# Attention by chunks of 512 queries, with the mixer, MLP and next projections of a finished chunk scheduled under the next chunk

## The chip, the core and the metric

The kernel runs on one core of a Trainium2 chip. The metric is device time in microseconds (us). The profiles are single executions. PE is the matrix engine, ACT the engine of exponentials and Gelu, DVE the vector engine, GpSimd (POOL) does small work, SP issues transfers. Attention is called bare where no side work runs under it. PSUM is the memory that PE writes; a bank of it holds one score tile.

A ratio below is the mean time of one kernel's runs over that of the kernel before, both from the same rounds. It is therefore not quite the ratio of the medians that are quoted.

## The reference, cut to what matters

Four layers over 2048 tokens of width 512: attention, mixer with MLP, attention, mixer with MLP. Attention has 32 query heads of width 16 and a single key and value head.

```python
def _A_ref(x, wq, wk, wv, wo):                      # H = 32, Dh = 16
    q = ...; k = x @ wk; v = x @ wv                 # one K and V for all heads
    scores = jnp.einsum("bhqd,bkd->bhqk", q, k) * (Dh ** -0.5)
    p = _softmax(scores, axis=-1)
    o = jnp.einsum("bhqk,bkd->bhqd", p, v)
    return o... @ wo
def _B_ref(x, w1, w2, w3, w4):
    h = _gelu(_layernorm(x) @ w1)
    ...                                             # four column groups shifted by 1, -1, 2, -2 tokens
    x1 = x + hs @ w2
    return x1 + _gelu(_layernorm(x1) @ w3) @ w4     # F = 1792
x = x + _A_ref(_layernorm(x), ...); x = x + _B_ref(_layernorm(x), ...)   # twice
```

There are 32 heads x 4 query chunks x 16 key blocks x 2 layers = 4096 score tiles of 128 x 512 to exponentiate. That is the largest single piece of work. A chunk's mixer needs only two tokens beyond the chunk, and its MLP nothing; only attention needs all keys.

## The kernel before

It works layer by layer. An attention step is one key block of three heads: three score matmuls on separate row groups of PE into three PSUM banks, one exponential over 1536 columns, four value matmuls on separate column groups. Two score slots alternate. Side work (Q projections, output projections, normalization) is slipped in by a fixed budget, one item in each step, through one PSUM bank.

```python
SBANK = [[0, 1, 2], [3, 4, 5]]
ACCB = 6
aux = {'b': 7, 'rot': None, 'i': 0, 'xb': 7}
...
for n in range(N):
    p, heads, qsb, kb = steps[n]
    emit_exp(n)
    ...                                   # fillers up to FILL_BUDGET = 0.55
    emit_pv(n, kb == NKB - 1)
    if n + 2 < N:
        emit_scores(n + 2)
```

After the last head of the last chunk the mixer layer follows, over all 16 token tiles. Gelu is built from a copy, a square and a tanh on ACT and two products on DVE, so that the exponential's activation table can stay.

```python
if kind == 'A':   # ACT copy of PSUM      'B': ACT Square      'D': ACT Tanh
...
sc.op("DVE", lambda e: e.scalar_tensor_tensor(out=un['dest'], in0=tb3, scalar=1.0, in1=pb3,
                                            op0=ALU.add, op1=ALU.mult), ...)
```

The softmax here doesn't subtract the row's maximum and nothing guards it: scores larger than these inputs give would overflow.

Of the kernel before, what the change touches and what calls it, by code (L numbers as in the profile page):

```python
# [12 lines left out]
class Sched:  # L13
    def __init__(self, nc):
        self.nc = nc
        self.thunks = {e: [] for e in ENGINES}
        self.count = {e: 0 for e in ENGINES}
        self.sems = {}
        for e in ENGINES:
            self.sems[e] = nc.alloc_semaphore(f"s_{e}")  # L20
        self.waited = {e: {} for e in ENGINES}
        self.res = {}
        self.subs = {}
        self.psum = {}
        self.ndma = 0
        self.out_dma_toks = []

    def _merge(self, deps, tok):
        if tok is None:
            return  # L30
        k, v = tok
        if deps.get(k, -1) < v:
            deps[k] = v

    def _tag_records(self, tag):
        zone, cell, sub = tag
        keys = [(zone, cell, None)]
        if sub is None:
            for s in self.subs.get((zone, cell), ()):
                keys.append((zone, cell, s))  # L40
        else:
            keys.append((zone, cell, sub))
        return keys

    def _deps(self, eng, reads, writes, banks):
        deps = {}
        for t in reads:
            for key in self._tag_records(t):
                info = self.res.get(key)
                if info is not None:  # L50
                    self._merge(deps, info['w'])
        for t in writes:
            for key in self._tag_records(t):
                info = self.res.get(key)
                if info is not None:
                    self._merge(deps, info['w'])
                    for k, v in info['r'].items():
                        self._merge(deps, (k, v))
        for b in banks:
            prev = self.psum.get(b)  # L60
            if prev is not None and prev[0] != eng:
                self._merge(deps, prev[1])
        return deps

    def _record(self, eng, tok, reads, writes, banks):
        for t in writes:
            zone, cell, sub = t
            if sub is not None:
                self.subs.setdefault((zone, cell), set()).add(sub)
            self.res[t] = {'w': tok, 'r': {}}  # L70
            if sub is None:
                for s in self.subs.get((zone, cell), ()):
                    self.res[(zone, cell, s)] = {'w': tok, 'r': {}}
        for t in reads:
            zone, cell, sub = t
            if sub is not None:
                self.subs.setdefault((zone, cell), set()).add(sub)
            info = self.res.setdefault(t, {'w': None, 'r': {}})
            k, v = tok
            if info['r'].get(k, -1) < v:  # L80
                info['r'][k] = v
        for b in banks:
            self.psum[b] = (eng, tok)

    def _emit_waits(self, e, eng, deps):
        for k, v in sorted(deps.items(), key=lambda kv: str(kv[0])):
            if self.waited[eng].get(k, -1) >= v:
                continue
            e.wait_ge(self.sems[k], v)
            self.waited[eng][k] = v  # L90

    def op(self, eng, emit_fn, reads=(), writes=(), banks=(), extra=()):
        reads = tuple(reads)
        writes = tuple(writes)
        banks = tuple(banks)
        deps = self._deps(eng, reads, writes, banks)
        for tok in extra:
            self._merge(deps, tok)
        self.count[eng] += 1
        tok = (eng, self.count[eng])  # L100
        if deps.get(eng, -1) >= tok[1]:
            raise AssertionError("self dependency")

        def thunk(e, deps=deps, emit_fn=emit_fn, eng=eng):
            self._emit_waits(e, eng, deps)
            ins = emit_fn(e)
            ins.then_inc(self.sems[eng], 1)
        self.thunks[eng].append(thunk)
        self._record(eng, tok, reads, writes, banks)
        return tok  # L110

    def dma(self, emit_fn, reads=(), writes=(), eng="SP", out=False, extra=()):
        reads = tuple(reads)
        writes = tuple(writes)
        self.ndma += 1
        key = f"d{self.ndma}"
        sem = self.nc.alloc_semaphore(key)
        self.sems[key] = sem
        deps = self._deps(eng, reads, writes, ())
        for tok in extra:  # L120
            self._merge(deps, tok)

        def thunk(e, deps=deps, emit_fn=emit_fn, eng=eng, sem=sem):
            self._emit_waits(e, eng, deps)
            ins = emit_fn(e)
            ins.then_inc(sem, 16)
        self.thunks[eng].append(thunk)
        tok = (key, 16)
        if out:
            self.out_dma_toks.append(tok)  # L130
        for t in writes:
            zone, cell, sub = t
            if sub is not None:
                self.subs.setdefault((zone, cell), set()).add(sub)
            self.res[t] = {'w': tok, 'r': {}}
            if sub is None:
                for s in self.subs.get((zone, cell), ()):
                    self.res[(zone, cell, s)] = {'w': tok, 'r': {}}
        for t in reads:
            info = self.res.setdefault(t, {'w': None, 'r': {}})  # L140
            k, v = tok
            if info['r'].get(k, -1) < v:
                info['r'][k] = v
        return tok

    def finish(self, block):
        outs = list(self.out_dma_toks)

        def final_thunk(e):
            for key, v in outs:  # L150
                e.wait_ge(self.sems[key], v)
        self.thunks["SP"].append(final_thunk)

        def mk(eng):
            def f(e):
                for t in self.thunks[eng]:
                    t(e)
            return f
        if self.thunks["PE"]:
            block.tensor(mk("PE"))  # L160
        if self.thunks["ACT"]:
            block.scalar(mk("ACT"))
        if self.thunks["DVE"]:
            block.vector(mk("DVE"))
        if self.thunks["POOL"]:
            block.gpsimd(mk("POOL"))
        if self.thunks["SP"]:
            block.sync(mk("SP"))


CELL = 1024


class Zone:
    def __init__(self, nc, name, nbytes, stack):
        assert nbytes % CELL == 0
        self.name = name
        self.nbytes = nbytes
        self.t = stack.enter_context(
            nc.sbuf_tensor(name, [128, nbytes // 2], dt.bfloat16))  # L180

    def view(self, byte_off, shape, dtype):
        esz = dt.size(dtype)
        n = 1
        for s in shape:
            n *= s
        assert byte_off % 4 == 0 and (n * esz) % 2 == 0
        ap = self.t[:, byte_off // 2: byte_off // 2 + (n * esz) // 2]
        if dtype != dt.bfloat16:
            ap = ap.bitcast(dtype)  # L190
        if len(shape) == 1:
            return ap
        dims = " ".join(f"a{i}" for i in range(len(shape)))
        kw = {f"a{i}": shape[i] for i in range(1, len(shape))}
        return ap.rearrange(f"p ({dims}) -> p {dims}", **kw)

    def cells(self, byte_lo, byte_hi, sub=None):
        assert 0 <= byte_lo < byte_hi <= self.nbytes, (self.name, byte_lo, byte_hi)
        c0 = byte_lo // CELL
        c1 = (byte_hi - 1) // CELL  # L200
        return [(self.name, c, sub) for c in range(c0, c1 + 1)]


class Buf:
    def __init__(self, zone, byte_off, shape, dtype):
        self.zone = zone
        self.off = byte_off
        self.shape = tuple(shape)
        self.dtype = dtype
        self.esz = dt.size(dtype)  # L210
        n = 1
        for s in shape:
            n *= s
        self.ap = zone.view(byte_off, shape, dtype)
        self.nbytes = n * self.esz
        st = [1] * len(shape)
        for i in range(len(shape) - 2, -1, -1):
            st[i] = st[i + 1] * shape[i + 1]
        self.strides = st

    def tags(self, *idx, sub=None):
        n_elems = 1
        for s in self.shape:
            n_elems *= s
# [16 lines left out]
class ZoneAlloc:  # L241
# [5 lines left out]
    def buf(self, shape, dtype, align=None):  # L247
# [3 lines left out]
        for s in shape:  # L251
            n *= s
# [871 lines left out]
```

## Time and profile before

2651.01 us (median of three, 2647.76 to 2652.38).

The five stages of this run (head, attention, mixer and MLP, attention, mixer and MLP) are cut out and timed in the prediction.

The page's forty slices show the stages at a glance: each digit is a tenth of the slice, PEclk the granted clock of PE.

```profile
PE   5888889888888889457878888888888888893588
...
ACT  5899999999999997346658999999999999973474
...
PEclk8955555555555555578988555555555555555789
```

ACT is near full where PE runs at half clock, and falls to 3 to 6 tenths where neither attention runs. The further lines of this profile stand in the prediction.

### The profile page before, as it was taken

The numbers are of one execution on the slowest core, as the hardware profiler recorded it, in microseconds if no ns is written. First come the engines' busy times: TensorE is split into PE (matmuls) and PEld (weight loads), VectorE is DVE, ScalarE is ACT, GpSimd is POOL, SyncE is SP. The second block draws the span as 40 slices with busy tenths as digits, with TensorE's granted clock in tenths as the row PEclk, the third lists the DMA queues.
The fourth block names the chain that finished last, engine by engine and source line by source line (L and its number), as shares of the span: only waits on it lengthen the run. The fifth ranks groups of instructions, "written<-read, shape, count | busy, mean of one in ns | idle before, by whom it ended". The sixth has DMA issues, their size and how long they took to land.

```text
span 2650.2 us, 30433 instructions
## 1 busy us (share of the span) xinstructions
PE 2174.1 (82%) x12641; PEld 550.5 (21%) x12728; DVE 842.9 (32%) x1552; ACT 2179.0 (82%) x1689; POOL 70.5 (3%) x93
## 2 busy tenths in 40 slices
PE   5888889888888889457878888888888888893588
PEld 2211111111111111123332111111111111110243
DVE  5312122012122012677742121220122121127776
ACT  5899999999999997346658999999999999973474
POOL 2000000000000000030100000000000000000200
PEclk8955555555555555578988555555555555555789
DMA  1000000000000000100000000000000000001000
GB/s 49 17 1 1 1 1 1 1 1 1 1 1 1 1 1 1 56 1 1 9 9 16 1 1 1 1 1 1 0 1 1 1 1 1 1 1 56 0 1 32
DMA packets 15466, 17.74 MB, mean 7 GB/s; under 512 B 2528, under 2 KB 14304, under 8 KB 15328
## 3 DMA queue, kind: packets, MB, share of 16 engines
q1 hardware_dynamic: 15328, 15.80, 1.9%
q8 instruction: 99, 1.62, 0.3%
q14 instruction: 39, 0.32, 0.0%
HBM read 13.70 MB, written 2.10 MB: 6 GB/s over the span
## 4 chain that ended last, share of the span: by engine, by line
ACT 47%; PE 35%; DVE 13%; issue 5%; DMA 0%; ACTq 0%; DVEq 0%
ACT zT L727 43%; PE PB L752 10%; PE PB L709 8%; PE PB L1021 4%; PE PB L689 4%; DVE zC L411 3%; PE PB L610 2%; DVE zT L771 2%; PE PB L734 2%; PE PB L1042 2%; DVE zT L618 2%; ACT zT L911 2%; PE PB L994 1%; DVE zT L816 1%; DVE zX L693 1%
## 5 line engine op out<-in xcount | busy, mean ns | idle before, releaser
L727 ACT ACTIVATE zT<-PB 128x1536 bf16<-128x1536 f32 (+1 forms) x1408 | 1926.2, 1411 | 193.9 <-PE PB L709 188.2
L752 PE MATMUL PB<-zT 128*32 128x512 bf16 x5632 | 849.7, 594 | 224.5 <-ACT zT L727 187.6
L709 PE MATMUL PB<-zT 32*128 32x512 bf16 x4096 | 837.4, 589 | 1.6 <-DVE zT L618 1.6
L771 DVE CAST zT<-PB 128x512 bf16<-128x512 f32 x88 | 60.6, 689 | 1118.8 <-PE PB L752 1118.8
L752 PEld LDWEIGHTS PB<-zT 128*32 128x32 bf16 x5632 | 155.8, 101 | 780.1 <-ACT zT L727 638.5
L709 PEld LDWEIGHTS PB<-zT 32*128 32x128 bf16 x4096 | 146.5, 98 | 596.3 <-issue 593.8
L693 DVE TENSOR_TENSOR zX<-PB,zX 128x512 f32<-128x512 f32 x256 | 176.4, 689 | 204.5 <-PE PB L689 170.2
L816 DVE TENSOR_TENSOR zT<-zT,PB 64x512 bf16<-64x512 bf16 (+2 forms) x144 | 98.7, 685 | 180.8 <-PE PB L800 179.0
L484 PE MATMUL PB<-zC,zT 128*128 128x128 bf16 x384 | 36.7, 274 | 132.1 <-ACT zT L461 108.5
L1021 PE MATMUL PB<-zW,zT 128*128 128x512 bf16 x440 | 112.2, 411 | 29.8 <-DVE zT L921 29.0
L689 PE MATMUL PB<-zW,zT 128*128 128x512 bf16 x212 | 124.5, 604 | 8.5 <-DVE zX L693 8.1
L908 ACT ACTIVATE zT<-PB 128x1024 bf16<-128x1024 f32 x72 | 74.1, 1029 | 64.1 <-PE PB L1042 53.1
L914 DVE SCALAR_TENSOR_TENSOR zT<-zT 128x1024 bf16<-128x1024 bf16 x72 | 88.2, 1225 | 79.8 <-ACT zT L911 79.8
L461 ACT ACTIVATE zT<-zT,zC 128x512 bf16<-128x512 f32 (+1 forms) x40 | 28.7, 801 | 102.4 <-DVE zC L449 102.4
L1042 PE MATMUL PB<-zT,zW 128*128 128x512 bf16 x438 | 101.0, 379 | 5.9 <-ACT zT L908 5.4
L921 DVE SCALAR_TENSOR_TENSOR zT<-zT 128x1024 bf16<-128x1024 bf16 x72 | 88.0, 1223 | 0.1
L461 ACT ACTIVATE zT<-zX,zC 128x512 f32<-128x512 f32 (+1 forms) x24 | 17.2, 801 | 81.6 <-DVE zC L449 81.6
L918 ACT ACTIVATE zT<-zT 128x1024 bf16<-128x1024 bf16 x72 | 76.6, 1064 | 4.4 <-DVE zT L914 4.4
L911 ACT ACTIVATE zT<-zT 128x1024 bf16<-128x1024 bf16 x72 | 76.7, 1065 | 0.0
L610 PE MATMUL PB<-zT,zW 128*128 128x512 bf16 x239 | 65.1, 391 | 10.4 <-DVE zT L618 2.9
L734 PE MATMUL PB<-zC 16*128 16x512 bf16 x88 | 51.6, 586 | 25.6 <-DVE zT L771 25.6
L800 PE MATMUL PB<-zC,zT 128*128 128x128 bf16 x352 | 67.6, 296 | 2.4 <-DVE zT L789 2.4
(68 smaller groups left out, 765.6 us busy)
## 6 DMA issues: line engine op xcount, KB each, us to landing
zW<-in_B_w_dram SPq DMA_DIRECT2D x4, 1792.0 KB, 9.5
zT<-in_A_x_dram SPq DMA_DIRECT2D x4, 512.0 KB, 5.5
zW<-in_B_w_dram SPq DMA_DIRECT2D x4, 512.0 KB, 3.5
out_dram<-zT SPq DMA_DIRECT2D x4, 512.0 KB, 3.2
zW<-in_A_wq_dram SPq DMA_DIRECT2D x2, 512.0 KB, 5.6
zW<-in_A_wo_dram SPq DMA_DIRECT2D x8, 128.0 KB, 2.6
zW<-in_A_wk_dram SPq DMA_DIRECT2D x2, 16.0 KB, 4.6
zW<-in_A_wv_dram SPq DMA_DIRECT2D x2, 16.0 KB, 2.1
```

Source lines behind the costliest of these rows:

```text
L610: ins = e.matmul(PB[:, bank, :], lhsT=WQB.ap[:, b, dc, :], rhs=YT.ap[:, dc, tc * 512:(tc + 1) * 512], start=(dc == 0), stop=(dc == 3))
L689: return e.matmul(PB[:, bank, :], lhsT=OT4.ap[:, b, tb * 128:(tb + 1) * 128], rhs=WO4.ap[:, b, :], start=True, stop=True)
L693: sc.op("DVE", lambda e: e.tensor_tensor(out=X32.ap[:, tb, :], in0=PB[:, bank, :], in1=X32.ap[:, tb, :], op=ALU.add), reads=X32.tags(tb), ...
L709: ins = e.matmul(PB[:, bks[j], :], lhsT=KTR.ap[32 * g:32 * g + 32, kb * 128:(kb + 1) * 128], rhs=QT.ap[32 * g:32 * g + 32, b, qsb * 512:(q ...
L727: return e.activation(ET[slot].ap[:, 0:nh, :], PB[:, b0:b0 + nh, :], ACTF.Exp, scale=0.25)
L734: return e.matmul(PB[:, ACCB, :], lhsT=INITL.ap[0:16, v, :], rhs=ONESR.ap[0:16, :], start=True, stop=False, skip_group_check=True)
L752: ins = e.matmul(PB[32 * g:32 * g + 32, ACCB, :], lhsT=VP.ap[:, kb, 0:32], rhs=ET[slot].ap[:, j, :], start=False, stop=(last_in_acc and ti ...
L771: sc.op("DVE", lambda e: e.tensor_copy(accf.ap, PB[:, ACCB, :]), writes=accf.tags(), banks=[ACCB])
L816: return e.tensor_tensor(out=OT4.ap[r0:r1, b, qsb * 512:(qsb + 1) * 512], in0=accf.ap[r0:r1, :], in1=PB[r0:r1, bank, :], op=ALU.mult)
L911: sc.op("ACT", lambda e: e.activation(sav, pbv, ACTF.Square, scale=float(np.sqrt(0.044715))), reads=pb.tags(), writes=sa.tags())
L1021: ins = e.matmul(PB[:, bank, :], lhsT=g2.ap[:, f, l * 128:(l + 1) * 128], rhs=W4B.ap[:, f, :], start=(f == 0), stop=(f == NFC - 1))
L1042: ins = e.matmul(PB[:, b0 + jj, :], lhsT=W3B.ap[:, dc, f * 128:(f + 1) * 128], rhs=ZT.ap[:, dc, tc * 512:(tc + 1) * 512], start=(dc == 0), ...
```

## The change

The intent: start the mixer, MLP and next K, V and Q of a chunk as soon as its 512 queries have been through all heads, and run them under the attention of the next chunk, so that ACT never leaves the exponentials for long. The whole program is declared as operations with durations and dependencies; a list scheduler places them in virtual time and so fixes the order on each engine, and the PSUM bank of each side operation. Score slots become 3 and 2 tiles wide, which leaves two banks for side work. Gelu becomes one instruction that needs another table. The second attention begins with the keys that exist (11 of 16 blocks) and spills partial sums.

```diff
+class Plan:
+    LAT = 0.13
+    SELF = 0.07
+    MARGIN = 0.35
...
+    def _pick(self, eng, t):          # ready operation of best priority; a side operation takes a free bank
...
+    ACT_SLOTS = ((0, 3), (3, 2))
+    ACC = 5
+    POOL_BANKS = (6, 7)
+    N_EA = 4
...
+        op("PE", fpe, reads=sorted(rd, key=str), writes=[("BK", b0)], dur=0.33, prio=0, side=False)
+        o = op("ACT", lambda e: e.activation(self.EA[:, ea, 0:n, :], self.PB[:, b0:b0 + n, :], ACTF.Exp,
+                                             scale=0.25),
...
+    def chunk_end(self, la, c):
+        for tb in tiles:
+            self.outproj(la, tb)
+        self.mixer_in(la, c, tiles, tail)
+        for tb in self.GR[c]:
+            self.mix(tb)
...
+            self.mlp(la, p, tail)
...
+        op("ACT", lambda e: e.activation(self.GP[:, par, :, 2:514], self.GP[:, par, :, 2:514],
+                                         ACTF.Gelu_apprx_tanh),
...
-        SBANK = [[0, 1, 2], [3, 4, 5]]
-        ACCB = 6
...
-            elif kind == 'B':
-                sc.op("ACT", lambda e: e.activation(sav, pbv, ACTF.Square, scale=float(np.sqrt(0.044715))),
```

## The prediction

> **What bounds the kernel now.** I cut the span into its five stages, at the first and last softmax exponential of each attention (the windows view; columns: from:to, length, busy us of PE, weight loads, DVE, ACT and GpSimd with instruction counts, granted TensorE clock, DMA share, GB/s).
>
> ```profile
> 0.00:33.80 33.80, 11.85 (x121) 8.45 (x123) 27.18 (x87) 7.04 (x10) 15.69 (x39) 1.00 0.32 95
> 33.80:1083.80 1050.00, 917.95 (x5480) 196.39 (x5505) 211.93 (x366) 962.25 (x703) 0.00 (x0) 0.54 0.01 2
> 1083.80:1351.80 268.00, 168.52 (x843) 79.80 (x859) 209.73 (x409) 126.79 (x141) 34.90 (x36) 0.79 0.06 18
> 1351.80:2402.00 1050.20, 921.72 (x5485) 196.65 (x5509) 207.18 (x351) 962.84 (x704) 0.00 (x0) 0.53 0.01 2
> 2402.00:2650.20 248.20, 154.02 (x719) 69.23 (x732) 186.93 (x340) 120.12 (x133) 19.89 (x18) 0.80 0.07 24
> ```
>
> Two attentions of 1050 us each keep ACT 92% busy at half the TensorE clock. The 268 and 248 us between and after them are mixer, MLP and layernorms, with ACT less than half busy: 516 us in which the exponential engine does little. That is what the change aims at. The groups by shape tell what an exponential costs (busy us, mean ns, idle before it and its releaser):
>
> ```profile
> L727 ACT ACTIVATE zT<-PB 128x1536 bf16<-128x1536 f32 x1280 | 1795.4, 1450 | 148.0 <-PE PB L709 144.8 <-ACT zT L727 2.3 <-PE PB L596 0.6
> L727 ACT ACTIVATE zT<-PB 128x1024 bf16<-128x1024 f32 x128 | 130.9, 1023 | 45.9 <-PE PB L709 43.3 <-ACT zT L727 0.3
> L752 PE MATMUL PB<-zT 128*32 128x512 bf16 x5632 | 849.7, 594 | 224.5 <-ACT zT L727 187.6
> L709 PE MATMUL PB<-zT 32*128 32x512 bf16 x4096 | 837.4, 589 | 1.6 <-DVE zT L618 1.6
> ```
>
> Whether ACT or PE sets the pace changes inside an attention. The timeline shows both cases (start, us, engine, line, operation). First bare attention at full clock, then a stretch with one output-projection matmul (L689) in each step:
>
> ```profile
> 125.10 0.40 PE L752 MATMUL PB<-zT 128*32 128x512 bf16 x4 [0.34 <-ACT zT L727]
> 125.43 0.39 PE L709 MATMUL PB<-zT 32*128 32x512 bf16 x3
> 126.44 0.40 PE L752 MATMUL PB<-zT 128*32 128x512 bf16 x4 [0.62 <-ACT zT L727]
> ```
>
> ```profile
> 342.06 0.61 PE L689 MATMUL PB<-zW,zT 128*128 128x512 bf16 x1
> 342.23 1.45 ACT L727 ACTIVATE zT<-PB 128x1536 bf16<-128x1536 f32 x1 [0.18 <-PE PB L709]
> 342.59 0.62 PE L752 MATMUL PB<-zT 128*32 128x512 bf16 x4
> 343.14 0.61 PE L709 MATMUL PB<-zT 32*128 32x512 bf16 x3
> 343.68 0.61 PE L689 MATMUL PB<-zW,zT 128*128 128x512 bf16 x1
> 343.86 1.45 ACT L727 ACTIVATE zT<-PB 128x1536 bf16<-128x1536 f32 x1 [0.18 <-PE PB L709]
> ```
>
> In the first, PE waits for ACT and a step takes 1.34 us: exponentials back to back, start to start 0.11 us less than the 1.45 us that one lasts. In the second, PE is never free: three batches 0.54 us apart make 1.63 us, ACT waits for each score. At full clock the same batches are 0.33 us apart (125.10 to 125.43). So the kernel is bound by ACT where attention is bare, by PE at half clock where work is slipped in, and by neither between attentions.
>
> The clock is the delicate part. The windows around its fall (same columns):
>
> ```profile
> 123.82:127.24 3.42, 2.39 (x23) 0.60 (x21) 0.69 (x1) 3.42 (x3) 0.00 (x0) 1.00 0.51 153
> 127.24:130.65 3.41, 1.62 (x18) 0.51 (x18) 0.00 (x0) 3.41 (x4) 0.00 (x0) 0.88 0.00 0
> 130.65:134.06 3.41, 2.96 (x21) 0.54 (x17) 0.00 (x0) 3.41 (x3) 0.00 (x0) 0.50 0.00 0
> ```
>
> Full clock lasts while four Q-projection matmuls sit in each step, and falls one window after they end. I then worked out for every 3.41 us window how full the array was: each 512-column stream counts 0.427 us at half and 0.213 us at full clock, times the share of rows and columns it uses (three score tiles are 0.75). Full clock was kept in windows above 0.36 and lost below 0.34. Half clock was kept up to 0.74 and left from 0.77 (three lower ones, 0.68 to 0.71, lie where matmul records are missing). The output-projection stretch above has (0.75 + 1 + 1) x 0.427 / 1.63 = 0.72, just short, which is why it stays slow although PE is never free.
>
> **What the Trainium skill says.** "TensorE: Matmul & The Clock Gate", Part 1: activity releases the throttle, the ratio is half or full only, the window is 3413 ns. The trace agrees: only 0.5 and 1.0 are granted, in multiples of 3.41 us. The page gives no activity threshold; the two above are mine. "TensorEngine Tiling (Array Packing)", Key Properties: changing the tiling mode drains the engine. The trace shows 0.54 against 0.43 us (half) and 0.33 against 0.22 (full) between batches, so some 0.11 us for each change. "ScalarE: Activation LUTs", What ACT_TABLE_LOAD costs: a load takes 1283 ns, with drain 2.66 us for each switch of set; this trace has one load, of 1283 ns, and no switch, so the drain is untested here. Same section: immediate-scale ACTIVATE 186 ns + 0.833 ns per column, overlapping by 93 ns; for 1536 columns 1.466 and 1.373 us, the trace has 1.450 and 1.34.
>
> **The change part by part.** Counts are from the instruction order of the changed kernel.
>
> 1. Exponentials. The 32 heads x 4 chunks x 16 key blocks x 2 layers are now cut in turns of 3 and 2 tiles: 819 of 1536 columns, 819 of 1024, one of 512, instead of 1280 and 128. Back to back: 819 x 1.335 + 819 x (1.023 - 0.115 = 0.908) + 0.5 = 1838 us. Before it would have been 1280 x 1.335 + 128 x 0.908 = 1825: nothing gained, 13 us lost; the third score bank went to the pool for side work. The zeroing matmul of each accumulation (88) goes.
>
> 2. Gelu. Copy, square, tanh and two DVE products (72 each: 74 + 77 + 77 us of ACT, 176 us of DVE) become 8 + 20 Gelu instructions. Of these 7 + 16 lie in the exponential stream: by 0.833 ns a column and about 0.06 us each, 7 x 1.77 + 6 x 2.3 + 8 x 3.05 + 2 x 1.55 = 54 us.
>
> 3. Table switches: 15 visits to Gelu within the stream, two loads each. With 1.28 us each 38 us, with the skill's 2.66 us 80; I take 45, as the drain overlaps the exponential's own end.
>
> ACT's stream is then 1838 + 54 + 45 = 1937 us without a stall.
>
> 4. Head: chunk 0 alone is needed for the first score, so the first exponential should come after the load (4.8 us), 4 stats, rstd on GpSimd, 4 normalizations, transposes, K, Q block 0: about 20 us, estimated from the durations of the present head (33.8 us). But 24 full matmuls per 5 tiles of score follow at once (K, V, Q of all chunks), so I add 20 us.
>
> 5. Tail: mixer and MLP of the last chunk stay outside: 32 output-projection, 16 + 20 mixer, 112 + 75 MLP matmuls at about 0.2 to 0.3 us (some 60 us) in a chain with DVE evacuations, stats, three Gelus and the last store: about 95 us, estimated, in place of 248.
>
> 6. Stalls in the stream. The order is lumpy: by 20 score tiles, half of the stretches hold hardly any side matmul, and 100 of 205 hold about 4 full matmuls per 5 tiles (up to 5). In a bare pair of exponentials (2.24 us), PE needs 2 score + 1.25 value batches, 3.25 x 0.54 = 1.76 us even at half clock: ACT-bound, perhaps 1% lost (10 us). In a dense pair at full clock PE needs 3.25 x 0.33 + 4.1 x 0.213 + some 0.17 of mode changes = 2.1 us of 2.24: nearly both bound, and a pair of side matmuls in front of a score costs a wait. I put 2.38 us: 400 x 0.14 = 56 us. At half clock it would be 1.76 + 1.75 + 0.17 = 3.7 us. The array share there is (0.53 + 0.53 + 1.75) / 3.7 = 0.76, at the threshold, so it should leave half clock within two or three windows; at full clock it is about 0.6, safe. With 11 dense stretches and some six dips in between I count 17 spells of about 8 us, each losing 35%: 50 us. Gelus waiting for their last evacuation: 15 us.
>
> Sum: 20 + 20 + 1937 + 95 + 10 + 56 + 50 + 15 = 2203 us; I say 2200. Seen from the stages: 268 of the middle goes, 153 of the tail, 14 of the head's first wait, and the attentions, 2100 us, end about where they were, since their present losses to half-clock projection (2100 - 1825) pay for the work taken in.
>
> **Rivals.** (a) PE becomes the bound because the clock stays at half in dense stretches: 400 x 1.3 = 520 us instead of 106, giving 2610, no gain. For it: 0.76 is at the edge and the present projection stretches never leave half clock. Against: a gap holds up to four side matmuls, which pushes single windows over 0.77. Partly so (a third of dense time cold): 2300. (b) The full 2.66 us switch and late Gelus, each holding ACT while both score slots are full: plus 35 to 60 us, 2250. (c) The planned order meets the chip almost without stalls, as its own durations suppose the full clock: 2203 less about 110, 2090. (d) DVE as bound: it falls from 843 us to an estimated 500, so no.
>
> **Range and chances.** (c) gives the low end, (a) partly true with (b) the high end: 2090 to 2340. Only (a) in full brings it back within 2%: 0.03; slower needs more than that: 0.01; faster 0.96.
>
> **What would show it.** Right: no stage without exponentials but head and tail; 819 + 819 exponentials of 1.45 and 1.02 us; ACT over 88% busy from 30 us to about 95 us before the end; clock 1.0 in dense and 0.5 in bare stretches; 32 loads of 1.28 us; tail of 80 to 110 us. Wrong: half clock through dense stretches, with ACT waiting for scores 0.54 us apart; more than 2 us lost around each switch beyond the loads; exponentials of 1024 columns well over 0.91 us start to start; a long wait where the second layer's first chunk needs the last keys.

## The result, and the profile after

2243.54 us (median of four, 2232.29 to 2245.48); the kernel before in the same runs 2651.7. Ratio 0.8454, interval 0.8433 to 0.8475. The forecast was 2200, its range 2090 to 2340.

The same slices, and the same cut at the first and last exponential (from:to, length, busy us of PE, weight loads, DVE, ACT, GpSimd with counts, granted clock, DMA share, GB/s):

```profile
PE   6777898878888798887879789887888878887867
...
ACT  2999998999999998999999989899998999899931
...
PEclk9555597755886578855689568765597756695568
```

```profile
0.00:21.40 21.40, 6.71 (x31) 3.07 (x31) 11.16 (x27) 1.30 (x2) 15.79 (x32) 1.00 0.93 307
21.40:2147.20 2125.80, 1790.87 (x11491) 457.56 (x11490) 432.06 (x819) 1977.89 (x1692) 44.31 (x90) 0.68 0.01 2
2147.20:2243.30 96.10, 66.69 (x315) 29.41 (x315) 42.31 (x86) 11.30 (x7) 5.59 (x11) 0.80 0.02 7
```

The two valleys of ACT are gone: one stream of 2126 us, 93% busy, with a head of 21 and a tail of 96 us. The clock now goes up and down with the side work. Two stretches of the second chunk show it, the first bare, the second with dense side work (same columns):

```profile
417.00:553.00 136.00, 111.76 (x670) 23.80 (x667) 9.23 (x18) 128.51 (x113) 0.00 (x0) 0.50 0.00 1
553.00:597.00 44.00, 40.26 (x312) 12.49 (x310) 20.90 (x39) 43.01 (x38) 3.33 (x6) 1.00 0.00 1
```

The exponentials by shape:

```profile
L646 ACT ACTIVATE EA<-PB 128x1536 bf16<-128x1536 f32 x819 | 1200.7, 1466 | 161.8 <-PE PB L695 87.1 <-PE PB L623 70.2
L646 ACT ACTIVATE EA<-PB 128x1024 bf16<-128x1024 f32 x819 | 854.1, 1043 | 4.8 <-PE PB L623 3.7
```

Nearly all the idle time of ACT lies before the wide exponentials, and more than half of it is put down to the value batch (L695), not to the scores (L623). That the scores of a wide one must come within the narrow one's 0.9 us may be why; the run with turns of three and three, below, bears on it.

Where the time goes, I worked out from each exponential's start to the next start. The shortest such step is 1.330 us after a wide and 0.904 us after a narrow one; what is more than that I call a stall. "Dense" means at least 1.3 side matmuls per 2.24 us (one wide and one narrow exponential, called a pair) nearby.

| term | forecast | measured |
|---|---|---|
| head to the first exponential | 20 | 21.4 |
| stalls in the first 50 us | 20 | 21.4 (one hole of 20.0) |
| exponentials back to back | 1838 | 1830.1 |
| Gelus and table loads in the stream | 54 + 45 | 97.4 |
| stalls, bare, half clock | 10 | 59.5 (0.143 per pair) |
| stalls, dense, full clock | 56 | 19.2 (0.068 per pair) |
| stalls, dense, half clock | 50 | 97.6 (0.947 per pair) |
| Gelu waiting for DVE's copies out of PSUM | 15 | none found in the stream |
| tail | 95 | 96.1 |

The sum of the stalls does not hang on what counts as dense, but the split does. Counted in five other ways (all side matmuls, only the larger ones, or each by its columns, within 4.5 or 6.7 us), half clock costs 40 to 80 us in bare and 77 to 117 us in dense stretches.

The two states of a dense stretch in the timeline (start, us, engine, line, operation), first at half clock, then 13 us later at full clock:

```profile
877.63 0.61 PE L623 MATMUL PB<-QT,KT 32*128 32x512 bf16 x3
878.17 0.62 PE L695 MATMUL PB<-EA,VP 128*32 128x512 bf16 x4
878.72 0.61 PE L623 MATMUL PB<-QT,KT 32*128 32x512 bf16 x2
878.84 2.37 ACT L646 ACTIVATE EA<-PB 128x1536 bf16<-128x1536 f32 x2 [1.47 <-PE PB L695]
879.26 0.62 PE L695 MATMUL PB<-EA,VP 128*32 128x512 bf16 x4
879.81 1.89 PE L946 MATMUL PB<-ZT,W 128*128 128x512 bf16 x4
```

```profile
890.48 0.39 PE L623 MATMUL PB<-QT,KT 32*128 32x512 bf16 x3
890.80 0.40 PE L695 MATMUL PB<-EA,VP 128*32 128x512 bf16 x4
891.13 0.60 PE L946 MATMUL PB<-ZT,W 128*128 128x512 bf16 x2
891.67 0.39 PE L623 MATMUL PB<-QT,KT 32*128 32x512 bf16 x2
```

At half clock batches follow 0.54 us apart without a gap, and ACT stands idle for 1.47 us; at full clock they are 0.33 us apart and ACT is not listed as waiting at all.

A visit to Gelu between exponentials looks like this:

```profile
333.76 1.28 ACT L885 ACT_TABLE_LOAD   x1
335.06 1.91 ACT L885 ACTIVATE GP<-GP 128x2048 bf16<-128x2048 bf16 x1
336.99 1.28 ACT L646 ACT_TABLE_LOAD   x1
338.28 3.28 ACT L646 ACTIVATE EA<-PB 128x1024 bf16<-128x1024 f32 x3
```

The instructions follow each other within 0.02 us. There is no room for a drain of more than a microsecond.

### The profile page after: what moved, and what is told of

Its sections match the earlier page's. It is cut to its first block, busy times and chain, and to the rows that moved or that the text cites. A ratio compares the mean times of both kernels' runs of the same rounds, so it can differ in the third digit from the quotient of the medians.

```text
span 2243.3 us, 26540 instructions
## 1 busy us (share of the span) xinstructions
PE 1864.3 (83%) x11836; PEld 490.0 (22%) x11836; DVE 485.5 (22%) x931; ACT 1990.5 (89%) x1699; POOL 65.7 (3%) x133
## 4 chain that ended last, share of the span: by engine, by line
ACT 59%; PE 36%; DVE 2%; POOL 1%; issue 1%; ACTq 0%; POOLq 0%
ACT EA L646 55%; PE PB L623 12%; PE PB L695 8%; PE PB L946 4%; PE PB L971 3%; PE PB L843 3%; PE PB L570 2%; ACT G L958 2%; PE PB L913 1%; PE PB L487 1%; ACT L646 1%; PE PB L877 1%; ACT GP L885 1%; PE PB L530 1%; PE PB L741 0%
## 5 line engine op out<-in xcount | busy, mean ns | idle before, releaser
L646 ACT ACTIVATE EA<-PB 128x1536 bf16<-128x1536 f32 (+1 forms) x1639 | 1883.4, 1254 | 166.6 <-PE PB L695 87.1
L623 PE MATMUL PB<-QT,KT 32*128 32x512 bf16 x4096 | 857.3, 518 | 257.3 <-ACT EA L646 252.9
L695 PE MATMUL PB<-EA,VP 128*32 128x512 bf16 x4096 | 545.5, 523 | 1.8 <-DVE ACCF L719 1.3
L623 PEld LDWEIGHTS PB<-QT,KT 32*128 32x128 bf16 x4096 | 164.4, 96 | 943.5 <-ACT EA L646 882.5
L695 PEld LDWEIGHTS PB<-EA,VP 128*32 128x32 bf16 x4096 | 110.7, 98 | 368.3 <-issue 357.7
L971 PE MATMUL PB<-W,G 128*128 128x512 bf16 x448 | 140.5, 436 | 52.9 <-ACT G L958 52.9
L946 PE MATMUL PB<-ZT,W 128*128 128x384 bf16 (+2 forms) x560 | 134.6, 364 | 1.5 <-DVE ZT L494 0.7
L951 DVE CAST G<-PB 128x512 bf16<-128x512 f32 (+2 forms) x140 | 81.7, 584 | 122.4 <-PE PB L946 121.5
L570 PE MATMUL PB<-YT,WQ 128*128 128x512 bf16 x256 | 83.0, 443 | 0.0
L843 PE MATMUL PB<-WO,OT 128*128 128x512 bf16 x256 | 72.3, 402 | 0.8 <-DVE OT L747 0.8
```

The costliest lines, as they stand in the source:

```text
L570: ins = e.matmul(self.PB[:, L.bank, :], lhsT=self.WQ[:, b, dc, :], rhs=self.YT[:, slot, dc, :], start=(dc == 0), stop=(dc == 3))
L623: return e.matmul(self.PB[:, bank, :], lhsT=self.KT[32 * h:32 * h + 32, la, kb * 128:(kb + 1) * 128], rhs=self.QT[32 * h:32 * h + 32, c % ...
L646: o = op("ACT", lambda e: e.activation(self.EA[:, ea, 0:n, :], self.PB[:, b0:b0 + n, :], ACTF.Exp, scale=0.25), writes=[("BK", b0), ("EA", ...
L695: ins = e.matmul(self.PB[32 * h:32 * h + 32, self.ACC, :], lhsT=self.VP[:, la, kb, :], rhs=e4[h][0], start=first, stop=(end is not None), ...
L843: ins = e.matmul(self.PB[:, L.bank, :], lhsT=self.OT[:, b, q:q + 128], rhs=self.WO[:, b, :], start=(b == 0), stop=(b == 7))
L946: ins = e.matmul(self.PB[:, L.bank, 0:n], lhsT=self.W3[:, dc, f * 128:(f + 1) * 128], rhs=ZT[:, dc, 0:n], start=(dc == 0), stop=(dc == 3))
```

## The experiments

Four questions were open: what made the 20 us hole in the head; whether the 157 us of half-clock stalls come from the clock or from the ring of four exponential buffers; what the table loads cost; and whether the overlap is what gained. Theory C holds that the half clock makes PE late; theory B that value batches, coming late, hold buffers which the next exponential needs. All kernels below give right results unless said otherwise, and each ran in three rounds beside the kernel before, which had medians of 2649.6 to 2651.6 us.

**V's weight first.**

```diff
-        load(self.W1, ..., 524288, 6)
+        load(self.W1, ..., 524288, 6, after=[("WV",)])     # and W2, W3, W4
```

> The four big weight loads wait until the small V weight has landed. Theory H (the 20.0 us hole of ACT between 25 and 46 us comes from V's weight queueing behind 4.7 MB of weights, so that the first value batches can't run and the four exponential buffers stay full): the hole shrinks to a few us, 2243 goes to about 2224 (-17 to -22 us), everything after it unchanged. Rival (the head's DVE and PE work fill those 20 us anyway): -8 us or less, the wait only moves to the keys of chunks 1 to 3.

2218.78 us, ratio 0.8366. Some 23 us less than the changed kernel by the ratios, a little more than expected. The hole of 20 us is gone; one of 7.0 us remains, in which ACT waits for scores. Theory H holds. The hole is the one of this line of the changed kernel, whose releaser is a value batch:

```profile
45.89 1.45 ACT L646 ACTIVATE EA<-PB 128x1536 bf16<-128x1536 f32 x1 [19.89 <-PE PB L695]
```

What is left of it in this run:

```profile
36.34 13.80 ACT L646 ACTIVATE EA<-PB 128x1536 bf16<-128x1536 f32 x12 [6.94 <-PE PB L623]
```

Value batches need V, V needs its weight of 16 KB, and that load was queued behind 4.7 MB of weights needed only 250 us later. My forecast's 20 us for the head were right in size, but I had put them down to PE being full of projections.

**Eight exponential buffers.**

```diff
-    N_EA = 4
+    N_EA = 8
```

> Eight exponential buffers instead of four. Theory B (part of ACT's waits before the 1536-column exponential is a buffer not yet read by a late value batch: 87 us are put down to the value batch, 20 of them in the head hole): -40 to -65 us, waits on the value batch nearly gone. Rival C (it is the half clock: PE is late with scores and values alike, a deeper buffer only moves the wait to the scores): within 15 us, the wait now put down to the score batch. The head hole may shorten by some 5 us under both.

2179.44 us, ratio 0.8227, 60 us less by the ratios (64 by the medians). Theory B's size is met. Idle time of ACT put down to the value batch falls from 87.1 to 9.5 us:

```profile
L646 ACT ACTIVATE EA<-PB 128x1536 bf16<-128x1536 f32 x819 | 1232.5, 1505 | 110.0 <-PE PB L623 98.3 <-PE PB L695 9.5
```

Stalls in bare stretches fall from 59.5 to 17.5 us (0.143 to 0.043 per pair), but in dense stretches at half clock they stay, 93.1 us (0.970 per pair). In the five other ways of counting, the bare ones fall by 34 to 45 us and the dense ones by 1 to 13. So each theory has its own part: the ring of four makes most of the bare stalls, something else the dense ones.

**Holding the clock.**

```diff
         self.units.append(o)
+        if k % 2 == 0:
+            D = Late()
+            def fd(e, D=D): ...      # two full 512-column matmuls, read by nobody
+            op("PE", fd, reads=[("W1",), ("W2",)], writes=[D], dur=t_mm(512, 2), prio=50, take=D, give=D)
```

> Adds 820 pairs of full 512-column matmuls of lowest priority, whose results nobody reads, placed where PE idles; results stay right. Theory C (158 us of stall at half clock, 0.143 us per pair in bare and 0.95 in dense stretches, against 0.07 at full clock in dense stretches, come from the clock): clock above 0.9 in nearly the whole stream, stalls before 1536-column exponentials fall to about 0.07 us per pair, 2243 goes to 2130 to 2165 (-80 to -115). Rival (the stalls are order and buffers, not clock; the added 350 us of matmul time costs as much as it gains): 2225 to 2270. If the array share needed to keep the clock is misjudged, the clock stays near 0.69 and the time rises by up to 40 us.

2182.61 us, ratio 0.8238. The gain of some 60 us falls between the two expectations. Mean clock 0.902 instead of 0.69. Dense stalls at half clock fall from 97.6 to 11.8 us, as theory C says. But in bare stretches one unread pair for two score batches is not enough to keep the clock: 71.0 us of stalls remain in the 355 us at half clock there, some 0.5 us per pair instead of 0.143. That the unread matmuls stand in the way there is likely, but was not shown. Bare pairs at full clock lose only 0.05 us, with the same four buffers: the ring costs much only at half clock.

**No table switch.** Its output is wrong, which doesn't matter for the time.

```diff
-ACTF.Gelu_apprx_tanh
+ACTF.Tanh
```

> Wrong result on purpose: Tanh in place of Gelu, which needs no other table, in the same order; 30 of the 32 table loads in the stream vanish. Theory S (ACT's stream is the bound, each visit costs two loads of 1.294 us and 0.13 us of lost overlap): -38 to -44 us. Rival (PE uses the pauses to catch up, so that the loads are partly free): -10 to -25 us.

2185.29 us, ratio 0.8246, 55 us less (by the ratios), above the range that I gave. Gelus and loads in the stream fall from 97.4 to 54.4 us, by 43.0, as theory S says: 30 loads, each with 0.13 us lost before it. The rest are stalls, 176.8 to 160.7 us after the first 50 us, mainly in dense stretches at half clock (97.6 to 77.0). Why those became fewer when the pauses became shorter was not tried by itself.

**V first and eight buffers.**

> V weight first and eight exponential buffers together. If the head hole (-23 us alone) and the late value batches (-60 us alone) are separate causes: 2160 to 2170, that is a ratio to the kernel before of 0.813 to 0.820. If the deeper buffer already covered part of the hole (its largest stall there is 9.6 us instead of 20.0): 2168 to 2178. The half-clock stalls of dense stretches (93 to 98 us in all) stay in either case.

2165.86 us, ratio 0.8174: 74 us less than the changed kernel by the ratios, where the two alone took 23 and 60. So they are largely separate causes, in the range for that; about half of the missing 9 us lies in the first 50 us, where eight buffers alone had already saved some 5 us of stalls. Dense half-clock stalls are still 79.4 us.

**The same, and an unread pair with every score batch.**

> As the run before, and a pair of unread full matmuls of lowest priority with every score batch (twice as many as in the earlier run, which still fell to half clock in bare stretches, 71 us of stall there). Theory C (what is left of the stalls is the half clock): clock above 0.95 in the stream, half-clock stalls of 110 us fall below 20, full-clock stalls 0.035 to 0.07 us per pair (28 to 57 us): 2085 to 2120. Rival (so many extra matmuls, some 1300, delay scores and side work as much as the clock gains): 2150 to 2180.

2253.63 us, ratio 0.8504: 88 us slower than the run before, and neither theory had named why. The windows up to and after the last exponential, and the second one cut once more where the last output has landed:

```profile
0.00:1985.00 1985.00, 1885.74 (x13607) 590.66 (x13845) 444.70 (x845) 1952.17 (x1693) 59.99 (x122) 1.00 0.02 6
1985.00:2250.50 265.50, 258.68 (x1247) 117.18 (x1269) 42.04 (x86) 11.25 (x6) 5.58 (x11) 1.00 0.01 3
1985.00:2076.00 91.00, 85.28 (x457) 38.40 (x464) 42.04 (x86) 11.25 (x6) 5.58 (x11) 1.00 0.02 8
2076.00:2250.50 174.50, 173.40 (x792) 78.78 (x806) 0.00 (x0) 0.00 (x0) 0.00 (x0) 1.00 0.00 1
```

In the stream theory C holds fully: clock 1.00, 25.3 us of stalls, last exponential 162 us earlier than in the changed kernel. But the scheduler had more unread pairs than places, and what was left over ran in the tail. It hardly held up the chain there: the last output landed at 2076.5 us, 91 us after the last exponential. The 174 us after that are unread matmuls alone. That was a fault of my experiment; without them the kernel would have taken about 2079 us, an estimate from this trace that was not run, and less than any run below.

**No overlap.** No exponential is started while work of a finished chunk, or a projection for a later one, is outstanding.

```diff
         while True:
+            ...                             # self.lagging: operations of priority 10, declared, not yet placed
+            if self.lagging:
+                break
             live = sum(1 for o in self.units[-4:] ...
```

> Undoes the overlap alone: no new exponential is started while work of a finished chunk is outstanding; chunks, Gelu instructions, buffers and the list scheduler stay. Theory (the gain is the overlap): each of the seven chunk ends inside the stream costs about what the last one costs in the open (96 us), less the Gelus and loads (14 us) and the dense stalls (17 us) already paid there: 2243 + 7 x 65 to 80 = 2700 to 2800, so as slow as the kernel before or slower. Rival (the gain is mostly the shorter Gelu and the better order): 2350 to 2500.

2716.43 us, ratio 1.0252: slower than the kernel before by some 67 us, in the range of the theory that the gain is the overlap. But this run hides less than the kernel before, which slips Q and output projections under its attention. Here they fill the first 13 to 17 us of each of the seven pauses, some 100 us in all, more than the 67 us. So without overlap nothing is left of the 400 us gained; that chunks, the shorter Gelu and the scheduler gain nothing by themselves is not shown. Time of the stream outside the exponentials rises from 97.4 to 607.7 us. The first exponential also comes later here (44.5 us), as the hold applies to the head's projections as well. This run's bare stretches also show the ring of buffers at its plainest (ACT alone, eight exponentials merged in a line):

```profile
378.32 9.14 ACT L647 ACTIVATE EA<-PB 128x1536 bf16<-128x1536 f32 x8 [0.35 <-PE PB L696]
387.81 9.14 ACT L647 ACTIVATE EA<-PB 128x1536 bf16<-128x1536 f32 x8 [0.35 <-PE PB L696]
```

Every eighth exponential waits 0.35 us for a value batch (here L696).

**Turns of three and three.**

```diff
-    ACT_SLOTS = ((0, 3), (3, 2))
-    ACC = 5
-    POOL_BANKS = (6, 7)
+    ACT_SLOTS = ((0, 3), (3, 3))
+    ACC = 6
+    POOL_BANKS = (7,)
```

> Turns of three and three score tiles as in the kernel before, leaving one PSUM bank instead of two for all side work; 1365 exponentials of 1536 columns. Base of the exponentials 1816 instead of 1830 us, and a score batch has 1.33 us instead of 0.90 to come, so bare stalls (59 us) should go: -70 us if side work can live on one bank. But one bank is full for about 2.3 us for every four matmuls, so dense stretches get thinner and longer, and by the array share (about 0.75 at half clock) leave half clock less readily: if that dominates, 2250 to 2350. I expect 2190 to 2300; under 2190 says that the 3 and 2 turn was a poor bargain.

2181.33 us, ratio 0.8226, below my expected 2190. Base of the exponentials 1816.4 us; stalls after the first 50 us are 69.5 instead of 176.8 us. One bank is enough for side work in the stream, but not in the head (a hole of 31.2 us) and the tail (142 us instead of 96). So the 3 and 2 turn of the change was a poor bargain with four buffers.

**Unread pairs with a cap of two waiting.** The cut is against the run with an unread pair with every score batch.

```diff
-        if k % 1 == 0:
+        self.idle_mm = [o for o in getattr(self, "idle_mm", ()) if not o.placed]
+        if k % 1 == 0 and len(self.idle_mm) < 2:
```

> As the run with V first, eight buffers and unread matmuls, but no more than two unread pairs may be waiting for a place, so that none are left over for the tail (there the stream ended at 1985 us, and the tail took 265 us instead of 96). Theory C: the stream ends at 1980 to 1995 us as before with the clock near 1.0, the tail is 96 us again: 2075 to 2100. If the unread matmuls themselves delayed the side work: the stream ends later, 2100 to 2140.

2109.8 us, ratio 0.796: 56 us less than without unread matmuls. But it is above the range of theory C and in its rival's, because the stream ends at 2017, not 1990 us. The trace shows why: without a backlog there are 14 spells of half clock in the stream instead of 3, all at the onset or in dips of dense stretches, with 35.3 us of stall. At full clock the stalls are small (0.028 bare, 0.034 dense per pair), so it is not that unread matmuls delay the rest, as the rival had it. The cap costs some 32 us in the stream against the run without it (2017 against 1985). The tail is 94 us.

**And five more banks in the tail.**

> The same, and after the last exponentials their five score banks are handed to the pool of side work, seven banks instead of two in the tail. If two banks limit the tail: -8 to -20 us. If the tail is a chain of layernorm, Gelu and evacuation: within 5 us.

2107.7 us, ratio 0.7952: the tail is a chain, two banks do not limit it (91 against 94 us). This is the fastest kernel, though not clear of the run before it, and beats both the kernel before and the changed one.

**Three and three with all repairs, without and with unread pairs.**

> Turns of three and three with one side bank (2181 us alone), with V first, eight buffers and six freed banks in the tail. Its profile alone shows a 31 us hole in the head, 31 us of waits on value batches and a tail of 142 us. Head -20, buffers -20 to -30, tail -40: 2085 to 2115. If the one bank is the cause of the head hole rather than V's weight, 2105 to 2135.

> The same with capped unread matmuls. Theory C: the half-clock stalls of dense stretches (49 us alone) go: 30 to 50 us less than without them, 2040 to 2080. Rival: the unread pairs occupy the only side bank, dense stretches get longer and the tail later: no better or slower, 2090 to 2140.

2127.78 us (ratio 0.8025) and 2119.97 us (ratio 0.799). The tail is 92 us with the freed banks, against 142: there one bank was the limit. In the head a hole of 15.5 us remains, so V's weight and the eight buffers together made about half of it; that the rest is due to the single bank was not shown. Eight buffers brought nothing in the stream (72.3 us of stalls against 69.5). Unread pairs removed the half clock in bare stretches, but not in dense ones (40.8 us against 43.9), as the rival said: 8 us gained instead of 30 to 50. That the single bank is the reason, as it had it, was not shown.

## Why the prediction was right or wrong

Direction, size and range were right, and 43 us are missing between 2200 and 2243. The table above has the terms. Part of the closeness is luck: the stalls of step 6 missed by 97 us one way and by 52 the other.

**Right.** What bounds the kernel (step 1 to 3): ACT's stream without stalls was put at 1937 us and is 1830.1 + 97.4 = 1927.5 us. The table loads take 1.28 us each with 0.13 us before each, so the small figure was the right one and rival (b) with its drain did not come. Head and tail came within 2 us. The view by stages, that the middle and most of the tail go and the attentions stay about as long, came out: the stream is 2126 us against 2100 of the two attentions. The clock does rise in dense stretches, but for about a third of their time it was still at half, with ACT waiting for batches 0.54 us apart: the sign that the prediction named as wrong, and the part of rival (a) that it put at 2300 us. In the changed kernel half clock was left from array shares of 0.72 on and kept up to 0.77; full clock was lost up to 0.37 and kept from 0.38 on. The two limits taken from the kernel before thus carried over to within some 0.03; the upper one is a band and not a line. Windows in which matmul records are missing read too low.

**Wrong: step 6, "ACT-bound, perhaps 1% lost (10 us)" in bare stretches.** It is 6%, 59.5 us. I had counted PE's time for a pair, 1.76 of 2.24 us, and checked that scores come in time; I had not asked when an exponential's output buffer comes free, which waits for a value batch that PE reaches late at half clock. With eight buffers the same stretches lose 17.5 us.

**Wrong in size: step 6, "17 spells of about 8 us, each losing 35%: 50 us".** The mechanism was right: holding the clock removed these stalls. But there were 35 half-clock spells in the stream after its first 50 us, and exponentials of dense stretches took 325 us in them, where 17 x 8 = 136 us had been supposed; the stalls are 97.6 us. I had counted the onsets and a few dips from the order of instructions in stretches of 20 tiles, some 9 us. The clock decides in windows of 3.41 us, and short spells were more frequent: 25 of the 35 lasted under 20 us.

**Wrong in size, the other way: dense at full clock, "400 x 0.14 = 56 us".** 19.2 us. At full clock a side pair in front of a score costs less than the wait that I had put there; and fewer pairs ran at full clock than I supposed. The 15 us for late Gelus were not needed: in the stream hardly any Gelu waited.

**Right in size for a wrong reason: "I add 20 us" in the head.** It was V's weight, late in its queue, as the first experiment shows, not the density of projections.

## What to carry to other kernels

When independent work is slid under a stage that one engine bounds, count first that engine's time without a gap, then ask of each of its instructions what it waits for: inputs, but also the buffer that it writes, whose reader may be slow for another reason. On PE the price of side work depends on how evenly it comes: in lumps it drops the clock between them and pays at each onset; filling the gaps, even with work that nobody reads, gained 56 us here; let none of it be left over for the end. And order loads by first use: a 16 KB load behind megabytes cost 20 us.

## What the Trainium skill lacked or had wrong

- "ScalarE: Activation LUTs", What ACT_TABLE_LOAD costs: it gives 2.66 us for each switch, with a drain of 1.38 us. Here a load took 1.28 us, and the exponential before it delayed it by 0.13 us (1.035 against 0.904 us start to start). Without the 30 loads the Gelu visits of the stream were 43.0 us shorter, 1.43 us a switch.
- Same section: it gives an overlap of 93 ns between instructions back to back. Exponentials of 1536 columns lasted 1.44 us at the least, 1.48 in the median, and started 1.330 us apart where nothing held them up, 0.11 us of overlap or more; the prediction's 1.373 us, an estimate from the page's figures, is 0.04 us too long.
- "TensorE: Matmul & The Clock Gate", Part 1: it gives the window and the two states but no threshold. Weighted by the share of rows and columns in use, full clock was lost in windows up to about 0.37 and half clock left somewhere between 0.72 and 0.77, in the trace of the changed kernel.
- Same page: its table "Why this matters for your kernels" advises to keep PE busy. It does not tell that batches of row and column tiles without a pause can stay at half clock: the output-projection stretches of the kernel before did, at a share of 0.72.
- "TensorEngine Tiling (Array Packing)", Key Properties: a change of mode drains the engine, without a figure. Here it cost 0.11 us at either clock (0.54 against 0.43, 0.33 against 0.22).
- On no page that I read: the GpSimd power operation that replaced the iterated root of the layernorm took 1.08 us for 128 x 4 elements (spans on GpSimd are rough).
